# Probabilities of batches 3 to 7 turned by transposing DMAs instead of TensorE, with one exponential for a group and normalisation moved into layer two

## The chip, the cores and the metric

The kernel runs on one core of a Trainium2 chip. The metric is the device time of one execution in microseconds. Three runs of the kernel before took 315.9, 316.6 and 315.95 us, median 315.95 us. TensorE (PE) multiplies matrices and writes to PSUM, its weight loads are listed apart (PEld); VectorE (DVE) and ScalarE (ACT) work on PSUM and SBUF; GpSimd (POOL) issues the loads here, and SyncE (SP) issues the stores and the transposing DMAs.

## The reference, cut to what matters

Sliding-window attention over 8 batches, 8 heads, 576 positions and 64 channels per head, followed by two matrix products with a SiLU between them.

```python
scores = scale * np.matmul(q, k.transpose(0, 1, 3, 2))
mask_plain = (rel >= 0) & (rel < 32)
mask_dil = (rel >= 0) & (rel < 128) & (rel % 4 == 0)
masks = np.stack([mask_plain if h < 4 else mask_dil for h in range(8)], axis=0)
scores = np.where(masks[None], scores, -1e9)
scores = scores - np.max(scores, axis=-1, keepdims=True)
attn = np.exp(scores)
attn = attn / (np.sum(attn, axis=-1, keepdims=True) + 1e-9)
attn_out = np.matmul(attn, v)
x = attn_out.transpose(0, 2, 1, 3).reshape(4608, 512)
h = x @ w_in                       # w_in is 512 x 2048
out = (h / (1 + np.exp(-h))) @ w_out   # w_out is 2048 x 512
```

## The kernel before

Each batch has 576 rows. Heads 0 to 3 use a window of 32 neighbours, "plain", z = 0 in the code; heads 4 to 7 use every fourth position back to 124, "strided", z = 1. Queries are cut into blocks of 32, keys into stretches of 64, and four blocks are stacked on the 128 partitions, so a probability tile `pe` or `pn` is 128 partitions by 8 or 10 slots of 64. For each batch and z there are two such tiles, hi = 0 and hi = 1: 8 and 10 slots for z = 0, 10 and 10 for z = 1. This is what is called a group here.

A group passes through these functions. `scores` (TensorE matmuls, then on VectorE the scaling and mask into `ms` and the negated maximum of each slot into `nm`); `exps` on ScalarE (for a group without `shift`, one exponential of 64 columns for each slot with the maximum as bias, which also gives the slot's sum `l`; for a group on which `shift` was called, VectorE has subtracted the maximum in place and one exponential covers all slots, line 525); `normal` on VectorE (line 543 sums the slots if the group was shifted, then line 547 adds epsilon, line 548 takes reciprocals `r`, line 550 writes `pn` in float16); `turn` (line 559: one TensorE transpose for each pair of slots, 4 or 5 for a tile, into PSUM tile `pt`); `turned` (line 567: a copy from PSUM to the SBUF tile `ptT`); `values` (lines 592 and 656: 64 or more small matmuls of `ptT` with the values `vw`); `finish` (lines 661 to 669: copies into `xT`, the transposed input of layer one).

The main loop goes over the batches. For batch b, `layer1` runs 16 blocks of 8 matmuls (line 682) with a SiLU after each on ScalarE (line 690); then `layer2` runs 4 output tiles for an even b and 5 for an odd b, each of 16 matmuls (line 747) with a copy `ob` on VectorE (line 731) and a store on SP (line 732). Attention of the batches that follow is woven into this. The order is written out by hand: `plan_of(b)` puts calls at steps, `plan(s)` runs those of step s. Steps 0 to 15 stand ahead of the 16 blocks of layer one. Steps 16 onwards stand ahead of every fourth matmul of layer two, so output tile x has steps 16 + 4x to 19 + 4x. Every engine executes its own instructions in this program order, and waits by semaphores.

For b of 2 and more the steps before are: the plain group of batch b + 1 is normalised at step 0, turned at 4 and multiplied with its values at 6 of layer one. Strided scores of b + 1 come at step 11 (10 for b = 2) and their exponentials at 16. Plain scores of b + 2 come at 17, their exponentials at 18. The strided group of b + 1 is normalised at 22 and 24 (hi = 0 and 1), turned at 27 and multiplied at 28 (28 and 29 for b = 6). Loads of values (`load_v`, `shift_v`) and of rows of q and k (`load_rows`) are issued on POOL; `cross` (lines 140 and 147) issues transposing DMAs on SP that put those rows into `qT`, `kT`, `qC` and `kC`. Buffers that matter: `ps` (4 PSUM tiles), `big` (2 PSUM tiles), `pt` (4), `pn` and `pe` (4), `ob` (5), `vw` (2).

The SP queue issues in program order, stores and transposes alike. A store that waits for its copy holds back what stands behind it.

Of the kernel before, what the change touches and what calls it, by code (L numbers as in the profile page):

```python
# [8 lines left out]
F16 = mybir.dt.float16  # L9
# [6 lines left out]
P = 128  # L16
# [13 lines left out]
def kernel(  # L30
# [9 lines left out]
    nc = tc.nc  # L40
    B, H, S, D = q.shape
# [15 lines left out]
    WM = 12  # L57
# [8 lines left out]
    ptp = ctx.enter_context(tc.tile_pool(name="ptp", bufs=4))  # L66
# [138 lines left out]
    def plain_v(a, j, h):  # L205
        return a["vw"][j % 2 * KB : j % 2 * KB + KB, h * NM + j // 2]

    def class_v(a, j, h, r):

        e = (j if j < 4 else h // 2) % 2  # L210
        return a["vw"][e * KB : e * KB + KB, NP + j // 2 * ND + h * DIL + r]
# [18 lines left out]
    def clear_v(b, engine):  # L230
# [13 lines left out]
        out=band[0:W], in_=band[0:W], compare_op=ALU.is_ge, fill=NEG,  # L244
# [3 lines left out]
        out=band[0:W], in_=band[0:W], compare_op=ALU.is_ge, fill=NEG,  # L248
# [35 lines left out]
    def att(b):  # L284
        if b not in state:
            state[b] = {
                "qT": qTs[b % 2],
                "kT": kTs[b % 2],
                "qC": qCs[b % 2],
                "kC": kCs[b % 2],  # L290
                "vw": vws[b % 2],
                "xT": xtp.tile([P, HP, S], F16, tag="xT", name=f"xT_{b}"),
            }
        return state[b]
# [87 lines left out]
    def width(b, z, g):  # L382

        if b == 0:
            return 8 + g * (4 if z else 2)
        return 10 if z or g else 8
# [176 lines left out]
    def turned(b, z, hi, copy=nc.vector.tensor_copy):  # L563
# [2 lines left out]
        pt = a["pt", z, hi] = ptp.tile([P, WM // 2, P], F16, tag="pt", name=f"ptT_{b}_{z}_{hi}")  # L566
        copy(pt[:, 0:n], a["ptT", z, hi][:, 0:n])  # L567

    def values(b, z):

        a = att(b)
        x = a["x", z] = [
            ps.tile([P, 2, SA], F32, tag="ps", name=f"x_{b}_{z}_{e}") for e in (0, 1)
        ]
        for i in range(8):
            for n in (0, 1):
                for e in (0, 1):
                    r = slice(e * KB, e * KB + KB)
                    for hi in (0, 1):
                        dst = x[e][hi * D : hi * D + D, n]  # L580
                        pt = a["pt", z, hi]
                        if z == 0:
                            j = 2 * i + e
                            w = plain_v(a, j, 2 * n + hi)
                            dst = dst[:, i * QB : (i + 1) * QB]
                            p = pt[r, 2 * n + j // 8, i % 4 * QB : i % 4 * QB + QB]
                        else:
                            m, c = i // 4, i % 4
                            w = class_v(a, 2 * m + e, 2 * n + hi, c)
                            dst = dst[:, m * P : (m + 1) * P].rearrange("d (i r) -> d r i", r=DIL)[:, c]  # L590
                            p = pt[r, 2 * n + m, c * QB : c * QB + QB]
                        nc.tensor.matmul(dst, w, p, start=True, stop=True)  # L592
        a["xs", z] = [
            ps.tile([P, 2, QB], F32, tag="ps", name=f"xs_{b}_{z}_{e}") for e in (0, 1)
        ]
        last_values(b, z, (0, 1))
# [163 lines left out]
    def transposes(at, b, z, step):  # L760
        for which in (1, 0):
            at(step, transpose, b, z, which, both)

    def later(at, b, z, steps, copies=(nc.vector.tensor_copy, nc.vector.tensor_copy)):

        for hi in (0, 1):
            if steps[hi] is not None:
                at(steps[hi], normal, b, z, hi)
        for hi in (0, 1):
            at(steps[2], turn, b, z, hi)  # L770
        for hi in (0, 1):
            at(steps[2], turned, b, z, hi, copies[hi])
        at(steps[3], values, b, z)
        at(steps[3], finish, b, z, copies)

    def plan_of(b):
        ev = {}

        def at(s, fn, *args):
            ev.setdefault(s, []).append((fn, args))  # L780

        def all_exps(b, z):
            for hi in (0, 1):
                at(16, exps, b, z, hi)

        if b == 0:

            at(-16, normal, 0, 1, 1)
            at(-15, shift_class, 0, dve, 1, 2)
            at(-14, normal, 0, 0, 1)  # L790
            at(-13, clear_v, 1, nc.vector)
            at(-13, load_v, 1)
            for c in (2, 3):
                at(-13, load_w_out, c)
            at(-13, load_qk, 2)
            at(-8, turn, 0, 1, 1)
            at(-8, turned, 0, 1, 1, act)
            at(-6, values0, 1, 1)
            at(-6, last_values, 0, 1, (1,))
            at(-6, finish0, 1, 1)  # L800
            at(-6, last_finish, 0, 1, 1)
            at(-4, turn, 0, 0, 1)
            at(-4, turned, 0, 0, 1)
            at(-2, values0, 0, 1)
            at(-2, last_values, 0, 0, (1,))
            at(-2, finish0, 0, 1, both)
            at(-2, last_finish, 0, 0, 1)
            transposes(at, 1, 1, 2)
            at(8, scores, 1, 1)
            for hi in (0, 1):  # L810
                at(8, shift, 1, 1, hi)
            for which in (1, 0):
                at(17, transpose, 1, 0, which, (dve, dve))
            at(20, normal, 1, 1, 0)
            at(20, scores, 1, 0)
            at(14, shift_v, 1, nc.sync.dma_start)
            at(15, load_rows, 3)
            at(15, load_v, 2)
            at(15, shift_v, 2, nc.gpsimd.dma_start)
            all_exps(1, 1)  # L820
            for hi in (0, 1):
                at(20, exps, 1, 0, hi)
            for n, z, hi in ((20, 1, 1), (26, 0, 0), (28, 0, 1)):
                at(n, normal, 1, z, hi)
            for n, z, copies in ((27, 1, (dve, dve)), (30, 0, both)):
                for hi in (0, 1):
                    at(n, turn, 1, z, hi)
                for hi in (0, 1):
                    at(n, turned, 1, z, hi, copies[hi])
                at(n + 1 + z, values, 1, z)  # L830
                at(n + 1 + z, finish, 1, z, both)
        elif b == 1:
            transposes(at, 2, 0, 2)
            transposes(at, 2, 1, 10)
            at(2, cross, 3, 0)
            at(20, cross, 3, 1)
            at(28, cross, 4, 0)
            at(7, scores, 2, 0)
            at(17, load_v, 3)
            at(17, shift_v, 3, nc.gpsimd.dma_start)  # L840
            at(17, load_rows, 4)
            at(13, scores, 2, 1)
            all_exps(2, 0)
            all_exps(2, 1)
            at(21, normal, 2, 0, 0)
            at(21, scores, 3, 0)
            at(21, exps, 3, 0, 0)
            at(21, exps, 3, 0, 1)
            later(at, 2, 0, (None, 24, 27, 28))
            later(at, 2, 1, (29, 31, 33, 34))  # L850
        else:
            if b + 2 < B:
                at(16, load_v, b + 2)
                at(16, shift_v, b + 2, nc.gpsimd.dma_start)
            if b + 1 < B:
                later(at, b + 1, 0, (0, 0, 4, 6))
                if b + 3 < B:
                    at(16, load_rows, b + 3)
            if b + 2 < B:
                at(20, cross, b + 2, 1)  # L860
            if b + 3 < B:
                for n, which in ((24, 1), (28, 0)):
                    at(n, cross, b + 3, 0, (which,))
            if b + 2 < B:
                at(17, scores, b + 2, 0)
                at(18, exps, b + 2, 0, 0)
                at(18, exps, b + 2, 0, 1)
            if b + 1 < B:
                at(10 if b == 2 else 11, scores, b + 1, 1)
                all_exps(b + 1, 1)  # L870
                later(at, b + 1, 1, (22, 24, 28, 29) if b == 6 else (22, 24, 27, 28))

        def plan(s):
            for fn, args in ev.pop(s, ()):
                fn(*args)

        return plan
# [58 lines left out]
    for b in range(B):  # L936
        plan = plan_of(b)
        if b == 0:
            for x in range(NFF):
                plan(2 * x - NFF)  # L940
                plan(2 * x + 1 - NFF)
                layer1_part(2 * x % NFF, 2 * x // NFF, None if x else warm)
        else:
            for f in range(NFF):
                plan(f)
                layer1(b, f)
        if b == 0:
            layer2_first(plan)
        else:
            layer2(b, plan)  # L950
        for s in range(NFF, 3 * NFF):
            plan(s)
# [30 lines left out]
```

## Time and profile before

| What | Value |
|---|---|
| Median of 3 runs | 315.95 us |
| The profiled execution | 316.03 us, its span 314.2 us |
| PE busy | 303.2 us, 96% of the span |
| ACT busy | 205.0 us, 65% |
| DVE busy | 164.5 us, 52% |
| POOL busy | 102.9 us, 33% |
| Granted TensorE clock | 1.00 |
| Layer two of batch 2 | first matmul at 119.58 us |
| Layer one of batch 3 | first matmul at 135.64 us |

The profile is of one execution. The times between the first and last instruction are the span; the rest of the 316.03 us lies outside it. In the chain of work that ended last, a line gives a start, a length and what ran. In a timeline a line gives start, length, engine, source line and operation; consecutive instructions of VectorE overlap a little at their ends, so a start can lie before the former line's end. "To landing" is the time from the start of a DMA's issue until its last semaphore update.

### The profile page before, as it was taken

Reading aid. Unit: us, or ns where it says so; the run is one execution under the profiler, and the core shown is the slowest. Engines: PE = TensorE matmul, PEld = TensorE weight load, DVE = VectorE, ACT = ScalarE, POOL = GpSimd, SP = SyncE. Lnnn points to the kernel's source line nnn. Section 1 sums busy time; section 2 is a strip of 40 time slices with the busy share of each in tenths; the row PEclk is TensorE's granted clock in tenths of the full one; section 3 lists DMA queues with packets and bytes.
Section 4 is the critical chain, followed back from the end, with each engine's and each line's share of the span. In section 5 each row is a group of like instructions: output and inputs, shape, how many; then the busy total and the mean of one; then the engine's idle time right before and its main releaser. Section 6 shows DMA issues by size and latency. Waiting matters only on the chain.

```text
span 314.2 us, 10664 instructions
## 1 busy us (share of the span) xinstructions
PE 303.2 (96%) x4551; PEld 196.0 (62%) x4551; DVE 164.5 (52%) x356; ACT 205.0 (65%) x683; POOL 102.9 (33%) x160
## 2 busy tenths in 40 slices
PE   5889999989999999999999999999999999999995
PEld 2658754667545875577644775567644775567544
DVE  5897488626497545742574545652574442520011
ACT  1775657756999559965796458965696458636300
POOL 8535537815582391147405570051000000000000
PEclk9999999999999999999999999999999999999999
DMA  8999999999999996699949991596042000210021
GB/s 106 182 214 205 193 231 175 160 182 152 135 161 208 197 110 81 164 166 143 115 109 164 211 112 26 150 161 122 5 104 106 35 2 2 96 41 2 0 100 67
DMA packets 93504, 38.45 MB, mean 122 GB/s; under 512 B 67665, under 2 KB 88017, under 8 KB 93457
## 3 DMA queue, kind: packets, MB, share of 16 engines
q0 software_dynamic: 64160, 21.73, 63.0%
q1 hardware_dynamic: 29152, 15.98, 21.8%
q8 instruction: 35, 0.57, 0.7%
q14 instruction: 13, 0.10, 0.1%
q10 hardware_dynamic: 144, 0.07, 0.1%
HBM read 37.75 MB, written 9.44 MB: 150 GB/s over the span
## 4 chain that ended last, share of the span: by engine, by line
PE 88%; ACT 4%; DMA 3%; DVE 2%; issue 1%; POOL 1%; POOLq 0%
PE h L682 35%; PE o L747 32%; PE o L721 5%; PE h L702 4%; PE x L592 3%; PE pt L559 3%; DMA n<-in_q_dram 2%; ACT pe L534 2%; PE s L362 1%; PE s L374 1%; PE t L312 1%; PE x L618 1%; POOL n L156 1%; PE xs L656 1%; DMA out_dram<-ob 1%
## 5 line engine op out<-in xcount | busy, mean ns | idle before, releaser
L690 ACT ACTIVATE gT<-h 128x576 f16<-128x576 f32 x112 | 73.0, 652 | 65.9 <-PE h L682 65.8
L747 PE MATMUL o<-w_out,gT 128*128 128x512 f16 (+1 forms) x528 | 114.9, 373 | 0.0
L682 PE MATMUL h<-xT,w_in 128*128 128x288 f16 x896 | 114.2, 286 | 0.0
L682 PEld LDWEIGHTS <-w_in 128*128 128x128 f16 x896 | 86.2, 98 | 23.1 <-DVE xT L669 0.3
L534 ACT ACTIVATE pe<-ms,nm 128x64 f32<-128x64 f32 x246 | 81.7, 337 | 4.2 <-DVE nm L502 4.2
L747 PEld LDWEIGHTS <-gT 128*128 128x128 f16 x528 | 50.4, 98 | 53.8
L731 DVE COPY ob<-o 128x512 f32<-128x512 f32 (+1 forms) x34 | 23.2, 682 | 58.8 <-PE o L747 57.8
L534 ACT ACTIVATION_READ_ACCUMULATOR pe<-ms,nm 128x1 f32 x246 | 47.0, 191 | 0.0
L486 DVE SCALAR_TENSOR_TENSOR ms<-s,mask 128x512 f32<-128x512 f32 x28 | 19.2, 686 | 45.1 <-PE s L374 25.0
L165 POOL DMA_DIRECT2D vw<-in_v_dram x16 | 10.0, 638 | 49.5 <-PE x L592 49.4
L550 DVE TENSOR_TENSOR pn<-pe,r 128x640 f16<-128x640 f32 (+2 forms) x32 | 25.3, 792 | 1.1
L669 DVE CAST xT<-x 128x512 f16<-128x512 f32 x26 | 16.8, 686 | 12.0 <-PE xs L656 12.0
L502 DVE TENSOR_REDUCE nm<-ms 128x10 f32<-128x640 f32 (+1 forms) x28 | 22.0, 787 | 1.0
L702 PE MATMUL h<-xT,w_in 128*128 128x256 f16 (+1 forms) x128 | 17.9, 296 | 0.5 <-ACT gT L709 0.5
L567 DVE COPY ptT<-pt 128x640 f16<-128x640 f16 (+1 forms) x28 | 12.1, 469 | 8.7 <-PE pt L559 8.7
L702 PEld LDWEIGHTS <-w_in 128*128 128x128 f16 x128 | 12.6, 101 | 4.6 <-issue 1.2
L721 PE MATMUL o<-w_out,gT 128*128 128x512 f16 x64 | 15.2, 380 | 0.2 <-issue 0.2
L119 POOL DMA_DIRECT2D n<-in_k_dram x20 | 14.9, 761 | 1.4 <-issue 1.3
L709 ACT ACTIVATE gT<-h 128x512 f16<-128x512 f32 (+1 forms) x16 | 10.3, 651 | 7.0 <-PE h L702 6.9
L119 POOL DMA_DIRECT2D n<-in_q_dram x20 | 14.8, 789 | 0.0
L559 PE MATMUL pt<-ident,pn 128*128 128x128 f16 x152 | 12.0, 224 | 0.4 <-DVE pn L550 0.4
L559 PEld LDWEIGHTS <-pn 128*128 128x128 f16 x152 | 10.1, 100 | 3.3 <-DVE pn L550 0.6
(108 smaller groups left out, 249.1 us busy)
## 6 DMA issues: line engine op xcount, KB each, us to landing
out_dram<-ob SPq DMA_DIRECT2D x35, 256.0 KB, 3.3
vw<-in_v_dram POOLq DMA_DIRECT2D x8, 288.0 KB, 8.0
vw<-in_v_dram POOLq DMA_DIRECT2D x16, 128.0 KB, 4.7
w_in<-in_moe_w_in_dram POOLq DMA_DIRECT2D x4, 512.0 KB, 11.9
w_out<-in_moe_w_out_dram POOLq DMA_DIRECT2D x4, 512.0 KB, 10.6
n<-in_k_dram POOLq DMA_DIRECT2D x6, 256.0 KB, 4.7
n<-in_q_dram POOLq DMA_DIRECT2D x6, 256.0 KB, 5.6
vw<-vw POOLq DMA_DIRECT2D x12, 128.0 KB, 3.3
```

The source lines that it names most:

```text
L119: nc.gpsimd.dma_start(out=f[:, h // 2, :, h % 2], in_=src[b, h].rearrange("(m p) d -> p m d", p=RT))
L486: nc.vector.scalar_tensor_tensor(out=ms[:, 0:8].rearrange("p (n t) c -> p n (t c)", n=2), in0=s[hi].rearrange("p n t c -> p n (t c)"), sca ...
L502: nc.vector.tensor_reduce(out=nm[:, 0:w], in_=ms[:, 0:w], axis=AX.X, op=ALU.max, negate=True)
L534: nc.scalar.activation(pe[:, t, :], slot(t), AF.Exp, scale=1.0 if b else scale, bias=nm[:, t : t + 1], accum_out=l[:, t : t + 1],)
L550: nc.vector.tensor_tensor(pn[:, 0:w], a["pe", z, hi][:, 0:w], r[:, 0:w, None].broadcast_to([P, w, KB]), ALU.mult)
L559: nc.tensor.transpose(t[:, i, :], a["pn", z, hi][:, 2 * i : 2 * i + 2].rearrange("p t c -> p (t c)"), ident)
L682: nc.tensor.matmul(h[:, half, 0:HS], w_in16[:, c, f * P : f * P + P], xT[:, c, half * HS : half * HS + HS], start=(c == 0), stop=(c == MC ...
L690: nc.scalar.activation(gT[:, f, s0 : s0 + S].rearrange("p (a c) -> p a c", a=2), h[:, :, 0:HS], AF.Silu)
L702: nc.tensor.matmul(h[:, i, 0 : c1 - c0], w_in16[:, c, (f + i) * P : (f + i + 1) * P], xT[:, c, c0:c1], start=(c == 0), stop=(c == MC - 1),)
L721: nc.tensor.matmul(o, gT[:, f, t * P : (t + 1) * P], w_out16[:, f, :], start=(f == 0), stop=(f == NFF - 1),)
L731: copy(ob, o)
L747: nc.tensor.matmul(o, gT[:, f, t * P : (t + 1) * P], w_out16[:, f, m0:m1], start=(f == 0), stop=(f == NFF - 1),)
```

## The change

For batches 3 to 7, `turn` and `turned` go away. A new function issues one transposing DMA on SP for each probability tile, straight from `pn` to `ptT`. The DMA has to wait for `pn`, and `values` for the DMA.

The strided group of b + 1 is still normalised at steps 22 and 24, each followed by its DMA, and `values` moves from 28 to 29. The plain group of b + 2 is normalised at steps 27 and 30 of layer two, each followed by its DMA, and `values` comes at step 4 of the next layer one. Batch 3's plain group is normalised and turned by DMA at step 0 of b = 2, and multiplied at 6. The hi = 1 tile of the strided group now has `shift` at step 11, so one exponential of 640 columns replaces ten of 64, and `normal` sums the slots on VectorE. In iteration 1, both tiles of batch 2's plain group are shifted in the same way at step 8, scores stand one step later, the exponentials of batch 3's plain group move from step 21 to 24. `cross` moves: the strided rows from step 20 to 16, the plain rows from 24 and 28 to 31.

```diff
+    def turn_by_dma(b, z, hi):
+
+        a = att(b)
+        w = width(b, z, hi)
+        pt = a["pt", z, hi] = ptp.tile([P, WM // 2, P], F16, tag="pt", name=f"ptT_{b}_{z}_{hi}")
+        nc.sync.dma_start_transpose(
+            out=pt[:, 0 : w // 2], in_=a["pn", z, hi][:, 0:w].rearrange("p t c -> p (t c)")
+        )
...
             transposes(at, 2, 0, 2)
-            transposes(at, 2, 1, 10)
+            transposes(at, 2, 1, 11)
...
-            at(7, scores, 2, 0)
+            at(8, scores, 2, 0)
+            for hi in (0, 1):
+                at(8, shift, 2, 0, hi)
...
-            at(13, scores, 2, 1)
+            at(14, scores, 2, 1)
...
-            at(21, exps, 3, 0, 0)
-            at(21, exps, 3, 0, 1)
             later(at, 2, 0, (None, 24, 27, 28))
+            at(24, exps, 3, 0, 0)
+            at(24, exps, 3, 0, 1)
             later(at, 2, 1, (29, 31, 33, 34))
         else:
             if b + 2 < B:
+                at(16, cross, b + 2, 1)
                 at(16, load_v, b + 2)
                 at(16, shift_v, b + 2, nc.gpsimd.dma_start)
+            if b + 3 < B:
+                at(16, load_rows, b + 3)
             if b + 1 < B:
-                later(at, b + 1, 0, (0, 0, 4, 6))
-                if b + 3 < B:
-                    at(16, load_rows, b + 3)
-            if b + 2 < B:
-                at(20, cross, b + 2, 1)
-            if b + 3 < B:
-                for n, which in ((24, 1), (28, 0)):
-                    at(n, cross, b + 3, 0, (which,))
+                if b == 2:
+                    for hi in (0, 1):
+                        at(0, normal, 3, 0, hi)
+                        at(0, turn_by_dma, 3, 0, hi)
+                at(6 if b == 2 else 4, values, b + 1, 0)
+                at(6 if b == 2 else 4, finish, b + 1, 0)
+                at(11, scores, b + 1, 1)
+                at(11, shift, b + 1, 1, 1)
+                all_exps(b + 1, 1)
             if b + 2 < B:
                 at(17, scores, b + 2, 0)
-                at(18, exps, b + 2, 0, 0)
-                at(18, exps, b + 2, 0, 1)
+                for hi in (0, 1):
+                    at(18, exps, b + 2, 0, hi)
             if b + 1 < B:
-                at(10 if b == 2 else 11, scores, b + 1, 1)
-                all_exps(b + 1, 1)
-                later(at, b + 1, 1, (22, 24, 28, 29) if b == 6 else (22, 24, 27, 28))
+                for hi in (0, 1):
+                    at(22 + 2 * hi, normal, b + 1, 1, hi)
+                    at(22 + 2 * hi, turn_by_dma, b + 1, 1, hi)
+                at(29, values, b + 1, 1)
+                at(29, finish, b + 1, 1)
+            if b + 2 < B:
+                for hi in (0, 1):
+                    at(27 + 3 * hi, normal, b + 2, 0, hi)
+                    at(27 + 3 * hi, turn_by_dma, b + 2, 0, hi)
+            if b + 3 < B:
+                at(31, cross, b + 3, 0)
```

## The prediction

> **What bounds the kernel now.** I read the page's busy table first, then the chain of work that ended last, then the chain's pieces over batches 2 and 3.
>
> ```profile
> PE 303.2 (96%) x4551; PEld 196.0 (62%) x4551; DVE 164.5 (52%) x356; ACT 205.0 (65%) x683; POOL 102.9 (33%) x160
> ...
> PE 88%; ACT 4%; DMA 3%; DVE 2%; issue 1%; POOL 1%; POOLq 0%
> ```
>
> ```profile
> 121.29 8.74 PE o L747 x40
> 130.03 0.56 PE pt L559 x10
> 130.59 0.86 PE o L747 x4
> 131.46 0.64 PE x L592 x64
> 132.10 0.14 PE xs L656 x16
> 132.24 3.56 PE o L747 x16
> ```
>
> TensorE is never idle here: piece follows piece. Whatever TensorE no longer does is gained in full, and whatever TensorE must wait for is lost in full. No other engine has a price of its own. So I look for what the new wait of `values` costs.
>
> Next, VectorE in the same stretch, which must finish `pn`, and the two kinds of transposing DMA on SP from 124 to 240 us (columns: shortest, median, longest issue in ns; below them the time from issue to landing).
>
> ```profile
> 127.48 0.69 DVE L731 COPY ob<-o 128x512 f32<-128x512 f32 x1 [1.00 <-PE o L747]
> 128.52 0.17 DVE L547 TENSOR_SCALAR r<-l 128x10 f32<-128x10 f32 x1 [0.35 <-ACT pe L534]
> 128.73 0.22 DVE L548 RECIPROCAL r<-r 128x10 f32<-128x10 f32 x1
> 128.98 0.82 DVE L550 TENSOR_TENSOR pn<-pe,r 128x640 f16<-128x640 f32 x1
> ```
>
> ```profile
> L147 SPq DMA_TRANSPOSE kC<-n x8: 1173/1224/1301, 125.5 to 232.1; - x8
> ...
> DMA to landing us min/median/max: 2.3/2.7/2.8
> ```
>
> ```profile
> L140 SPq DMA_TRANSPOSE kT<-n x6: 1220/1650/2462, 131.4 to 204.2; - x6
> ...
> DMA to landing us min/median/max: 4.2/5.7/8.4
> ```
>
> The first kind runs while POOL loads nothing, the second from the moment the next values are loaded. The same instruction takes 2.3 to 2.8 us in quiet and 4.2 to 8.4 us beside loads.
>
> **Removed from TensorE.** Five batches lose ten transposes (0.56 us in the chain, as above) and nine (0.50 us, at 139.72 us and alike in the others): 5 x 1.06 = 5.3 us gained. VectorE's copies `ptT` (0.4 to 0.5 us each) go too; VectorE is 52% busy, so nothing comes of it by itself.
>
> **Strided group, steps 22 to 29, five times.** `normal` of hi = 1 stands at step 24, in program order behind the copy `ob` of output tile 1, which waits for that tile's last matmul. In layer two of batch 2 this copy starts at 127.48 us. An independent VectorE operation behind a 0.69 us one starts 0.60 us later (the pair at 122.61 and 123.21 us), so the new slot sum starts at 128.08. It takes 0.82 us (813 ns in its row of the page's groups, 128x10 from 128x640), to 128.90. Then lines 547, 548 and 550 need 1.28 us, as from 128.52 to 129.80 above: `pn` is ready at about 130.21, SP issues at 130.26.
> The landing is unknown for 128x5x128. In quiet the 128x8x128 transpose of 125.47 us issued for 1.27 us, moved 1,024 rows of 256 bytes until about 1.0 us after that, and had landed 2.75 us after its start. With 5 of 8 tiles the middle part is 0.64 us: 2.35 us, which I take, as it is nearest in kind. Lower end 1.9 us, if the issue shrinks by 5/8 also; upper end 2.75 us. Landed and seen: 132.66.
> TensorE arrives at step 29 after 48 matmuls of 0.216 us from 121.23 us (first matmul behind the plain scores), with 0.1 us for the switch of shape: 131.70. So it waits 0.95 us, five times: 4.75 us (ends 2.5 and 6.75). The tile hi = 0 has `pn` at 126.5 us and is hidden. The single exponential (732 ns for 128x640 in line 525's row, against 3.3 us for ten) saves ScalarE 2.6 us, but ScalarE waits for TensorE, 65.8 us of it at line 690, so this is worth nothing; the subtraction that it adds on VectorE (0.82 us in layer one) is hidden by VectorE's idle time there.
>
> **Plain group of batch 3.** It has no earlier place: `pn` is ready at 103.54 and 104.74 us in the trace of before, SP is held 1.25 us by the first transpose, so the second starts at 104.85. POOL is loading values then. Stores issued at 100.94 and 102.53 us landed after 5.3 and 4.8 us, the quickest transpose beside loads took 4.2: I take 4.5, landing 109.35, seen 109.4. TensorE comes to step 6 at 101.61 + 6 x 0.98 + 0.1 = 107.6: a wait of 1.8 us (0 with 2.75 us, 3.8 with 6.5 us).
>
> **Plain groups of batches 4 to 7.** `pn` of hi = 1 follows the copies into `xT`. From the end t of the values: copies 1.5 us, normalisation 1.28 us, issue at t + 2.8. TensorE needs it at step 4, after 12 matmuls (2.6 us) and 4 blocks (3.9 us): t + 6.6 for even b. Up to 3.75 us of landing is hidden. POOL starts its loads at t, in bursts; the first `kT` beside them landed after 4.2 to 4.5 us, one in quiet would after 2.35. I take 4.0, which gives 0.2 us each for batches 4 and 6: 0.4 us together (0 and 7.4). For odd b four more steps of layer two hide 7.2 us: nothing (upper end 1.2 us each).
>
> **Iteration 1.** VectorE's order is `ob`, the slot sum of hi = 0, its `pn`, the masks of batch 3, `ob`, the slot sum of hi = 1, its `pn`. ScalarE's earlier end pays for the first sum: in the trace VectorE waited 0.6 us for `pe` there. The second sum adds 0.73 us (820 ns less overlap) ahead of `pn`, while line 547 shrinks by 0.16: TensorE's turn at 90.66 us, which already waited 0.6 us for `pn`, waits 0.55 us more (0 and 1). Shifts at step 8 lie in idle time of VectorE.
>
> **The queue.** SP now issues four more transposes of 1.2 us an iteration, 4.9 us of some 35. Behind a waiting transpose stand stores; five `ob` buffers cover a delay of some microseconds. Strided `cross` moves ahead of POOL's loads into layer one, its readers come at step 11 of the next iteration. Plain `cross` at step 31 is read at step 17, over 15 us later. Both cost nothing unless SP hangs back by a layer.
>
> **Sum.** -5.3 + 4.75 + 1.8 + 0.4 + 0.55 = +2.2 us on the profiled execution's 316.03 (span 314.2, 1.8 around it): 318.2. That execution lies 0.08 us over the median of 315.95, which changes no digit that matters.
>
> [...] Beside loads the traces show transposes landing up to 8.4 us after issue. [...]
>
> **Rivals.**
> [...]
> Faster: the issue shrinks with the tile count. Then a quiet landing takes 1.9 us, each strided wait is 0.5 us, and the plain landings lose the same 0.45: 2.5 + 1.35 + 0 + 0.55 - 5.3 = -0.9, 315.1; with a gap in the loads for batch 3, 313.8. It decides once the quiet landing is under some 1.95 us. Against it: 128x8x16, an eighth of the data, still issued for 1.17 us and landed after 2.3.
> Heavy queues: plain transposes land as the `qT` ones beside loads did (six of them, 6.1 to 8.4 us; I take 7): batch 3 waits 4.3 us, batches 4 and 6 3.2 us each: -5.3 + 4.75 + 4.3 + 6.4 + 0.55 = +10.7, 326.7 us. For it: qT issued at 135.63, about when the new one would be, took 7.5 us. Against it: that one stood behind two `kT`, which now come after.
> The change not doing what it says: the transposes leave TensorE by construction; only the waits are open.
>
> **How the numbers follow.** A difference of 0.3% (0.95 us) is about what a measurement tells from none. My sum 0.45 (317 to 320.5), fair turns 0.15 (same), faster 0.20, heavy queues 0.20 (320.5 to 327, fewer the higher). So faster 0.20, same 0.15, slower 0.65. The time is 318.2; the range 314.2 to 323.2 leaves out about half of the faster case and half of the heavy one.
>
> **What would show it.** In the profile after: L559 has 57 instead of 152 transposes; TensorE has a gap of about 0.95 us ahead of `values` in layer two of batches 2 to 6, ended by a DMA `ptT`; one of some 1.8 us at block 6 of batch 2; the new DMA lands 2.2 to 2.5 us after issue in quiet. If the gaps in layer two are under 0.5 us or the DMA is quicker than 2 us, I am wrong to the fast side; if gaps at block 4 of batches 3 and 5 exceed 1.5 us, to the slow side.

## The result and the profile after

The changed kernel takes 329.0 us (median of four runs, 326.97 to 332.25) against 315.92 us for the kernel before in the same job: a ratio of 1.0388 with a 95% interval of 1.0338 to 1.0438. The forecast was 318.2 us with a range up to 323.2. The sign was right, the size was not: +13 us came, +2.2 were forecast.

The ratio leaves out the profiled execution, which at 332.25 us (span 330.5) is the longest of the four and 3.3 us above their median, so its waits are a little long; the lower clock is not its own alone (0.978, against 0.972 to 0.983 in the other three). First the page of the changed kernel: the busy row, the granted TensorE clock in 40 slices of 8.26 us, and the chain that ended last by engine.

```profile
PE 304.7 (92%) x4456; PEld 194.7 (59%) x4456; DVE 166.3 (50%) x350; ACT 186.4 (56%) x554; POOL 102.7 (31%) x160
...
PEclk9999999999999789999999999995999999999999
...
PE 79%; DMA 12%; DVE 3%; ACT 3%; issue 1%; POOL 1%; POOLq 0%
```

TensorE has 95 matmuls fewer and yet no less busy time than before (304.7 against 303.2 us). DMA holds 12% of the chain in place of 3%, and the clock row shows three slices below 9. The page of before has none.

The instructions and waits around the tile `ptT` in the changed kernel, for the new DMA alone (durations of the issue in ns, who waited for it in us and times, then the time from issue to landing):

```profile
L574 SPq DMA_TRANSPOSE ptT<-pn x20: 1193/1207/1232, 104.0 to 287.9; - x20
...
  PE x L601: 14.9, 9
...
DMA to landing us min/median/max: 2.3/2.4/7.7
```

TensorE waits for the new DMA nine times, 14.9 us in all. The median landing is the 2.35 us of the forecast; the longest is three times that.

**Strided groups.** TensorE in layer two of batch 2 of the changed kernel (start, length, what ran, and in brackets the idle time ahead):

```profile
138.88 0.21 PE L601 MATMUL x<-ptT,vw 64*64 64x32 f16 x1
139.91 0.70 PE L601 MATMUL x<-ptT,vw 64*64 64x32 f16 x63 [0.82 <-DMA ptT<-pn]
```

From the first matmul, which needs hi = 0 only, to the second one, which needs hi = 1, it is 1.03 us. The other four places have 1.01 or 1.02. This is the 0.95 of the forecast.

**Plain group of batch 3.** TensorE in layer one of batch 2, changed kernel:

```profile
105.80 1.51 PE L691 MATMUL h<-xT,w_in 128*128 128x288 f16 x11
110.93 0.17 PE L601 MATMUL x<-ptT,vw 64*64 64x32 f16 x1 [3.62 <-DMA ptT<-pn]
113.01 1.04 PE L601 MATMUL x<-ptT,vw 64*64 64x32 f16 x63 [1.91 <-DMA ptT<-pn]
...
114.09 7.04 PE L691 MATMUL h<-xT,w_in 128*128 128x288 f16 x40
```

The two turns were issued at 103.98 and 105.28 us and landed after 6.90 and 7.68 us, so TensorE stands still from 107.2 to 113.0 but for one matmul, 5.75 us beyond its usual pace. And then 40 matmuls of layer one take 7.04 us. The same 40 in the kernel before, in layer one of batch 5:

```profile
213.51 0.69 PE L592 MATMUL x<-ptT,vw 64*64 64x32 f16 x64
...
214.19 5.07 PE L682 MATMUL h<-xT,w_in 128*128 128x288 f16 x40
```

The windows of the changed kernel say why (columns: stretch, us, PE busy with count, granted clock, DMA share, GB/s):

```profile
107.00:111.30 4.30, 0.48 (x4) 1.00 1.40 123
111.40:118.10 6.70, 5.09 (x88) 0.50 1.74 198
118.20:121.00 2.80, 2.80 (x24) 1.00 1.45 129
...
224.00:230.70 6.70, 6.34 (x94) 0.50 1.21 192
```

The clock falls inside the long wait, at 111.3 us, and is 0.50 for 6.8 us; TensorE works for 5.1 us of these. (The last row is from the wait of batch 6, below.) In batch 3 the fall follows 3.7 us without the start of a matmul (107.24 to 110.93 us) and then a single one; in batch 6, at 223.94 us, it comes 3.4 us after the last matmul ended. The clock is back after 6.83 us both times, 5.1 and 6.3 us of them work. What sets these lengths no run shows. The prediction did not think of it.

**Plain group of batch 6**, layer one of batch 5, changed kernel:

```profile
220.36 0.20 PE L601 MATMUL x<-ptT,vw 64*64 64x32 f16 x1
224.36 1.04 PE L601 MATMUL x<-ptT,vw 64*64 64x32 f16 x63 [3.80 <-DMA ptT<-pn]
...
225.44 9.63 PE L691 MATMUL h<-xT,w_in 128*128 128x288 f16 x56
```

The same picture: 4.0 us of waiting, then 56 matmuls in 9.63 us, where they take 7.03 at full clock (in the experiment with the filled wait). The plain group of batch 4 waited 1.79 us (landing 5.39 us after its issue) and lost no clock; that of batch 5 needed 6.23 us and was covered by the fifth output tile.

The difference of the two profiled executions, 330.48 - 314.23 = 16.25 us, by the starts of the stages:

| Step of the forecast | Forecast | Measured |
|---|---|---|
| Transposes gone from TensorE | -5.3 | -5.3 (0.50 less in each layer one without a wait: 17.37 against 17.87) |
| Five strided waits | +4.75 | +5.0 |
| Plain, batch 3 | +1.8 | +8.0: 5.75 of wait, 1.97 of half clock in the 40 matmuls, the rest in the slower small ones |
| Plain, batches 4 and 6 | +0.4 | +1.8 and +7.0 (4.0 of wait, 2.6 of half clock in the 56 matmuls, the rest in the small ones) |
| Iteration 1 and all before batch 2 | +0.55 | -0.3 (+0.7 in the wait for `pn`, the rest elsewhere) |
| Sum | +2.2 | +16.2 |

### The profile page after: what moved, and what is told of

Its sections match the earlier page's. It is cut to its first block, busy times and chain, and to the rows that moved or that the text cites. A ratio compares the mean times of both kernels' runs of the same rounds, so it can differ in the third digit from the quotient of the medians.

```text
span 330.5 us, 10385 instructions
## 1 busy us (share of the span) xinstructions
PE 304.7 (92%) x4456; PEld 194.7 (59%) x4456; DVE 166.3 (50%) x350; ACT 186.4 (56%) x554; POOL 102.7 (31%) x160
## 3 DMA queue, kind: packets, MB, share of 16 engines
q0 software_dynamic: 64160, 21.73, 61.3%
q1 hardware_dynamic: 41952, 19.10, 26.9%
## 4 chain that ended last, share of the span: by engine, by line
PE 79%; DMA 12%; DVE 3%; ACT 3%; issue 1%; POOL 1%; POOLq 0%
PE h L691 32%; PE o L756 29%; DMA ptT<-pn 10%; PE o L730 4%; PE h L711 4%; PE x L601 3%; DMA n<-in_q_dram 2%; PE s L374 1%; PE s L362 1%; PE t L312 1%; PE pt L559 1%; ACT pe L534 1%; PE x L627 1%; POOL n L156 1%; PE xs L665 1%
## 5 line engine op out<-in xcount | busy, mean ns | idle before, releaser
L691 PE MATMUL h<-xT,w_in 128*128 128x288 f16 x896 | 117.9, 293 | 0.0
L691 PEld LDWEIGHTS <-w_in 128*128 128x128 f16 x896 | 88.5, 100 | 25.9 <-DVE xT L678 0.3
L534 ACT ACTIVATE pe<-ms,nm 128x64 f32<-128x64 f32 x178 | 59.1, 333 | 4.2 <-DVE nm L502 4.1
L534 ACT ACTIVATION_READ_ACCUMULATOR pe<-ms,nm 128x1 f32 x178 | 33.1, 186 | 0.0
L601 PE MATMUL x<-ptT,vw 64*64 64x32 f16 x896 | 12.0, 192 | 14.9 <-DMA ptT<-pn 14.9
L601 PEld LDWEIGHTS <-vw 64*64 64x64 f16 x896 | 9.9, 114 | 20.7 <-issue 20.7
L711 PEld LDWEIGHTS <-w_in 128*128 128x128 f16 x128 | 12.8, 103 | 4.4 <-issue 0.8
L186 POOL DMA_DIRECT2D vw<-vw x6 | 2.9, 489 | 22.6 <-DMA vw<-in_v_dram 22.6
```

The costliest lines, as they stand in the source:

```text
L534: nc.scalar.activation(pe[:, t, :], slot(t), AF.Exp, scale=1.0 if b else scale, bias=nm[:, t : t + 1], accum_out=l[:, t : t + 1],)
L691: nc.tensor.matmul(h[:, half, 0:HS], w_in16[:, c, f * P : f * P + P], xT[:, c, half * HS : half * HS + HS], start=(c == 0), stop=(c == MC ...
L711: nc.tensor.matmul(h[:, i, 0 : c1 - c0], w_in16[:, c, (f + i) * P : (f + i + 1) * P], xT[:, c, c0:c1], start=(c == 0), stop=(c == MC - 1),)
```

## The experiments

Theory after the result: the turns that are issued while POOL loads values land late, because of the loads; the rest is the half clock. Rivals: the strided waits, the single exponential, or the order on SP.

**One part alone.** The plain groups are turned on TensorE as before, the strided ones by DMA.

```diff
-                if b == 2:
-                    for hi in (0, 1):
-                        at(0, normal, 3, 0, hi)
-                        at(0, turn_by_dma, 3, 0, hi)
-                at(6 if b == 2 else 4, values, b + 1, 0)
-                at(6 if b == 2 else 4, finish, b + 1, 0)
+                later(at, b + 1, 0, (0, 0, 4, 6))
...
-                for hi in (0, 1):
-                    at(27 + 3 * hi, normal, b + 2, 0, hi)
-                    at(27 + 3 * hi, turn_by_dma, b + 2, 0, hi)
```

> The plain groups of batches 3 to 7 are turned on TensorE again (normalised at step 0, turned at 4, values at 6, as before); the strided ones stay with DMAs. Theory: all of the loss beyond some 2 us comes from the plain groups, whose DMAs share the queues with the loads of values, and from the half clock after their long waits. Then 5 strided waits of 1.0 us against 5 turns of 0.56 us saved: 315.9 + 2.2 - 0.3 (iteration 1, as the trace of the changed kernel has it) = 317.8 us, clock 1.00. Rival: transposing DMAs hold up SP and the rest of the queues in any place, half of the loss stays: 322 us or more.

Measured: 320.63 us, ratio 1.013 (1.0084 to 1.0176). The waits of TensorE in this kernel (us in total, times, longest):

```profile
PE x L601 <- DMA ptT<-pn: 4.1, 5, 0.9
...
PE s L374 <- issue: 3.1, 3, 1.4
```

The five strided waits are there, but the kernel is 2.8 us over the expectation, and what stands beside it is called "issue": TensorE waits for nothing that the profile shows. More of that below.

The other part alone: strided groups back on TensorE, plain ones by DMA.

```diff
-                for hi in (0, 1):
-                    at(22 + 2 * hi, normal, b + 1, 1, hi)
-                    at(22 + 2 * hi, turn_by_dma, b + 1, 1, hi)
-                at(29, values, b + 1, 1)
-                at(29, finish, b + 1, 1)
+                later(at, b + 1, 1, (22, 24, 28, 29) if b == 6 else (22, 24, 27, 28))
```

> The other half alone: the strided groups are turned on TensorE at 27, values at 28 (28 and 29 for b = 6), the plain ones by DMA as in the changed kernel. Theory: the changed kernel's 327 to 329 us less 5 x 0.44 = 325 to 327 us, clock still 0.97 to 0.98. Rival: the two halves disturb one another through the SP queue, and one alone goes well: under 320 us.

Measured: 330.11 us, ratio 1.0417 (1.036 to 1.0474), no better than the whole change. From issue to landing its ten turns take

```profile
DMA to landing us min/median/max: 2.5/5.7/8.4
```

The expectation was 325 to 327 us, so this is missed by 3 us: with the strided groups back on TensorE nothing was regained in the total. The plain groups carry the loss.

**The half clock by itself.** Twelve matmuls of 512 columns on idle data stand ahead of the plain values in the layer one of batches 2 and 5; they fill part of the wait and move nothing else.

```diff
+                if b in (2, 5):
+                    at(6 if b == 2 else 4, fill, 12)
                 at(6 if b == 2 else 4, values, b + 1, 0)
```

> The changed kernel with 12 matmuls of 128x512 on an unused PSUM tile (12 x 0.216 = 2.6 us) ahead of the plain values in layer one of b = 2 and b = 5, inside the waits of 5.7 and 4.3 us. Theory of the clock: the idle stretch gets shorter than what makes the clock fall to 0.50, the waits end when they did, and the slow matmuls behind them (2.0 and 2.6 us lost) go: 328 - 4.6 = 323.4 us, mean clock 0.99 or more. Rival: the time behind the waits was lost to something else, such as buffers: 328 us as before, or more.

Measured: 326.66 us, ratio 1.0307 (1.0235 to 1.0379), against 323.4 expected. The timeline of TensorE in this kernel, first for batch 3, then for batch 6, and a window from the stretch that had a clock of 0.50:

```profile
107.16 2.75 PE L911 MATMUL fill<-ident 128*128 128x512 f16 x12
109.88 0.17 PE L601 MATMUL x<-ptT,vw 64*64 64x32 f16 x1
111.10 0.68 PE L601 MATMUL x<-ptT,vw 64*64 64x32 f16 x63 [1.05 <-DMA ptT<-pn]
...
111.78 5.07 PE L691 MATMUL h<-xT,w_in 128*128 128x288 f16 x40
```

```profile
220.46 7.03 PE L691 MATMUL h<-xT,w_in 128*128 128x288 f16 x56
```

```profile
113.50:118.00 4.50, 4.50 (x112) 1.00 2.10 119
```

The 40 and the 56 matmuls are back at 5.07 and 7.03 us, the clock at 1.00: the half clock follows from the idle wait, and costs 1.97 + 2.60 us in these matmuls. The profiled execution, 324.68 us, is below the median here; in it the landings were also shorter (batch 3: 6.56 and 6.48 us), so not all of the 7.6 us to the profiled execution of the change are the clock's. The medians differ by 2.3 us only.

**What holds the landings.** First without any loads and shifted copies of values for batches 4 to 7.

```diff
-                at(16, load_v, b + 2)
-                at(16, shift_v, b + 2, nc.gpsimd.dma_start)
```

> The changed kernel without the loads of values for batches 4 to 7 and the shifted copies made of them (lines 165 to 198 from b = 2 on); the matmuls then use the values of batches 2 and 3. TensorE's instructions are the same, one for one. Theory: the plain DMAs land late because of these loads. Without them they land after 2.3 to 2.5 us, as the strided ones do; batch 3 waits 0.5 us, batches 4 and 6 not at all, the clock stays at 1.00: 315.9 - 5.3 + 5.0 + 0.5 + 0.7 (iteration 1) = 316.8 us. Rival: the transposes on SP hold one another up (four for q and k stand behind each plain pair); landings stay over 5 us, the time over 324 us. A side question: TensorE's waits named issue sum to 4.9 and 8.4 us in the two runs that came out slower than expected, against 2.2 before. If they are instruction blocks that come late beside loads, they fall to 2 us here.

Measured: 326.38 us, ratio 1.0261 (1.0174 to 1.0349), against 316.8 expected. The new DMA in this kernel between 98 and 116 us, and between 210 and 235:

```profile
L574 SPq DMA_TRANSPOSE ptT<-pn x2: 1226/1833/2440, 102.7 to 105.3; - x2
DMA to landing us min/median/max: 8.8/9.0/9.3
```

```profile
L574 SPq DMA_TRANSPOSE ptT<-pn x3: 1205/1207/1309, 210.8 to 216.8; - x3
DMA to landing us min/median/max: 2.3/2.4/2.7
```

In the later batches the theory holds: without the loads the plain turns land like quiet ones, and the waits of batches 4 and 6 are gone (layer one of batch 5 takes 17.49 us instead of 24.36). Batch 3 became worse, and that the theory had not foreseen: with its value work gone POOL comes to the loads of q and k rows sooner, at 93 to 106 us where they were issued at 111 to 119, and those arrive in pieces of 128 bytes too. What harms is not values as such.

So next only one load was left out, the one of line 178, which brings the plain values in pieces of 128 bytes.

```diff
-                at(16, load_v, b + 2)
+                at(16, load_v, b + 2, ("first", "second", "short"))
```

> The changed kernel without one of the five value loads, that of line 178 (36 x 64 pieces of 128 bytes), for batches 4 to 7. Theory: this one, with 2304 short packets, holds the transposes up: landings of the plain DMAs fall to 2.4 to 4 us, time 317 to 319 us. Rival: the longer packets (512 bytes of lines 165 and 173, 4096 of the shifted copies) do as much: landings stay over 5 us, time 324 us or more.

Measured: 318.92 us (ten runs), ratio 1.0039 (0.9994 to 1.0085). The turns of batch 3 in it:

```profile
L574 SPq DMA_TRANSPOSE ptT<-pn x2: 1195/1286/1378, 105.2 to 106.5; - x2
DMA to landing us min/median/max: 4.2/4.2/4.2
```

The turn of batch 4 lands after 3.65 us, that of batch 5 after 2.65 in place of 6.23. One load of 288 KB for each of four batches, with its 128-byte pieces, makes ten microseconds of the change's thirteen. SP's order is the same in both kernels. The DMA queues of the changed kernel from 104 to 106.9 us show what it does (q0 carries POOL's loads, 64,160 packets on the pages of before and after; q1 what SP issues, 29,152 before and 41,952 after; packets, MB, share of 16 engines):

```profile
q0 software_dynamic: 1947, 0.32, 145.5%
q1 hardware_dynamic: 192, 0.31, 29.8%
```

Nearly two thousand small packets of q0 run in these 2.9 us, and only 8 of the 256-byte packets of the turn that was issued at 103.98; those came from 107 us on, some 300 to 390 a microsecond. That q0 goes first is read from this trace, not tested by itself.

**The single exponential.** Without the shift of the strided hi = 1, ten exponentials again, and VectorE has no slot sum ahead of `pn`.

```diff
-                at(11, shift, b + 1, 1, 1)
```

> The changed kernel without the shift at step 11, so that the strided hi = 1 group has ten exponentials again and no slot sum in normal. Theory: the slot sum (0.82 us) stands in the chain copy of tile 1, sum, normalisation, DMA, values; without it ScalarE's tenth exponential sets the start, 128.52 in the trace of before, where the sum let it start at 128.93. The strided waits fall from 1.0 to about 0.6 us. Rival: nothing changes there, since VectorE is late for another reason: 1.0 us.

Measured: 325.82 us, one execution. The strided gaps shrink to 0.58 to 0.63 us in four places, as expected: the sum on VectorE ahead of `pn` costs 0.4 us each. The fifth, in layer two of batch 6, grows to 1.39. The plain gaps stay (3.65 + 1.59, 1.20, 3.05 us), so the exponential is not the cause of the loss.

**Values later.** If only the landing is late, `values` can come later: plain ones at step 14, strided ones at 30.

```diff
-                at(6 if b == 2 else 4, values, b + 1, 0)
-                at(6 if b == 2 else 4, finish, b + 1, 0)
+                at(14, values, b + 1, 0)
+                at(14, finish, b + 1, 0)
...
-                at(29, values, b + 1, 1)
-                at(29, finish, b + 1, 1)
+                at(30, values, b + 1, 1)
+                at(30, finish, b + 1, 1)
```

> The changed kernel, with the plain values moved from steps 4 and 6 to 14 and the strided ones from 29 to 30. Theory: every landing then lies under TensorE's work. The plain ones have 8 to 10 us more, which covers the longest seen (7.7 us); the strided ones 0.87 us more, against a wait of 1.0: 0.1 us left each. 315.9 - 5.3 + 0.5 - 0.3 = 310.8 us, clock 1.00. Rival: the later values collide with the masks on VectorE (four PSUM tiles are shared with the strided scores of step 11) or keep the next layer one waiting for its input: 313 us or more.

Measured: 320.69 us, ratio 1.0137 (1.009 to 1.0184). The theory's 310.8 us was missed by ten; the rival's "313 us or more" came true, but its reasons (VectorE, the next layer one's input) account for 1.4 us at most, the waits for `ob`. All landings are hidden now; the waits of TensorE in this kernel are others:

```profile
PE x L601 <- issue: 2.1, 2, 1.1
PE s L362 <- issue: 2.0, 1, 2.0
PE h L691 <- DVE ob L740: 1.4, 2, 0.7
...
PE o L756 <- issue: 1.0, 1, 1.0
```

One of them in its timeline, in the middle of 64 equal matmuls whose operands were all there:

```profile
152.74 0.55 PE L601 MATMUL x<-ptT,vw 64*64 64x32 f16 x45
154.43 0.33 PE L601 MATMUL x<-ptT,vw 64*64 64x32 f16 x19 [1.14 <-issue]
```

I numbered TensorE's instructions in the traces (matmuls, weight loads and the few others of its queue, such as waits for a semaphore, in order of start, from 0). For five of the kernels, the last instruction ahead of each "issue" gap of over 0.9 us behind instruction 2000, with the gap from start to start in us:

```
kernel                      number (gap)
before                      2496 (1.17)
after                       2752 (0.98)
plain on TensorE            2752 (1.32)  4032 (1.64)
values 14, 30               2496 (2.17)  4288 (0.94)  5056 (1.32)  5312 (1.35)  6080 (1.15)
without line 178's load     2240 (1.02)  2496 (1.35)  5312 (1.22)
```

Every number is 192 more than a multiple of 256 (why 192 stays open). The traces of before and after also show 35 transfers of 16,384 bytes each on an instruction queue of their own (the pages' q8: 35 packets, 0.57 MB), one for about every 256 of TensorE's 9,125 and 8,931 instructions. In the kernel with 14 and 30 one starts at 152.1 us, the gap begins at 153.1 and ends at 154.4. My reading, from these counts and places alone: each transfer brings a block of 256 instructions, and where TensorE is through with its 256 before the next block has come, it waits. Scores and values are quick ones: with the values at 14, close behind the scores at 11, blocks pass in 3.9 to 4.2 us, while in the kernel before, with layer-one matmuls between them, none takes under 4.87. The limit is not sharp: gaps follow blocks of 4.9 to 8.0 us too, where the transfer started late, 3.5 to 5.8 us behind the last border.

To test this, the same kernel with 72 narrow transposes on idle data in iteration 1, ahead of the turn that waits there anyway. They move every later block border by 144 instructions, and no work.

```diff
+        for _ in range(72 if (b, z, hi) == (2, 0, 1) else 0):
+            nc.tensor.transpose(t[:, 0, 0:32], ident[0:32], ident[0:32, 0:32])
         for i in range(width(b, z, hi) // 2):
```

> The values at steps 14 and 30, with 72 narrow transposes more on TensorE (144 instructions with their weight loads) in iteration 1, ahead of the turn that waits there 1.41 us anyway; what they write is overwritten. Theory (instructions come in blocks): with the values at 14 and 30 alone every stall of over 0.9 us named issue stands at a TensorE instruction whose number is 192 more than a multiple of 256 (2496, 4288, 5056, 5312, 6080), and it stands where a whole block of 256 passes in under about 5.3 us. Moved by 144, hardly a block after 95 us passes so fast (the shortest in that trace would take 5.6 us), so the stalls at 121.96, 153.11, 160.12 and 192.00 go (4.8 us, with the small ones up to 7); the 72 cost about 1.9 us less the wait of 1.41. Time 314 to 317, about 315.5, against 320.7. Rival (the stalls belong to the work at their places, a semaphore or a port): they stay at the same matmuls, time about 321.

Measured: 314.56 us (nine runs), ratio 0.9952 (0.9925 to 0.9979). It does more work than the kernel without them and is 6 us faster. The extra instructions, and the values that had a gap in their middle, in its timeline:

```profile
90.37 1.96 PE L559 MATMUL pt<-ident 32*128 32x32 f16 x72
...
151.06 0.68 PE L603 MATMUL x<-ptT,vw 64*64 64x32 f16 x64
```

None of the four gaps after 95 us is left. Instead of moving the borders, the work can be pulled apart: strided scores from step 11 to 5, plain values from 14 to 12.

```diff
-                at(14, values, b + 1, 0)
-                at(14, finish, b + 1, 0)
-                at(11, scores, b + 1, 1)
-                at(11, shift, b + 1, 1, 1)
+                at(12, values, b + 1, 0)
+                at(12, finish, b + 1, 0)
+                at(5, scores, b + 1, 1)
+                at(5, shift, b + 1, 1, 1)
```

> The values at 14 and 30 with the strided scores moved from step 11 to 5 and the plain values from 14 to 12, so that seven layer-one tiles stand between them. Theory (blocks): no block is made of scores and values alone, so the stalls of the iterations at 153.11, 160.12 and 192.00 go (3.8 us); the landings of the plain turns are hidden still, but for batch 3 (landed about 13 steps after its issue: 0 to 1 us). Time about 316 to 317.5. Rival (the stalls belong to the work): about 320.7 as with 14 and 30.

Measured: 313.99 us (ten runs), ratio 0.9932 (0.9898 to 0.9966), better than expected. No "issue" gap of over 0.5 us is left after 76 us.

A third use of the same idea, the first experiment with its strided values at step 30:

```diff
-                at(29, values, b + 1, 1)
-                at(29, finish, b + 1, 1)
+                at(30, values, b + 1, 1)
+                at(30, finish, b + 1, 1)
```

> Plain groups turned on TensorE as before, strided groups by DMA with their values at step 30 in place of 29. With step 29 the five waits for the landing took 5.11 us; one step later is 0.87 us of matmuls, so 0.15 us each is left at most. Theory (each wait is a plain term): 320.6 - 4.4 = 316.2, within 0.3% of before. Rival (the waits hid other work, blocks of instructions or VectorE): 318 or more, with the time back under issue or pn.

Measured: 317.8 us, ratio 1.0033 (0.9998 to 1.0067), between the two. No wait for the strided turns is left in TensorE's list, but gaps stand at 4032 (2.09 us) and 7104 (1.29 us), both 192 beyond a multiple of 256. Behind the first one the clock fell too, for 3.4 us, although the wait was short:

```profile
113.00:116.40 3.40, 1.50 (x85) 1.00 1.55 128
116.50:119.80 3.30, 3.30 (x16) 0.50 0.53 115
```

**The order on SP.** The kernel with 14 and 30, with the strided `cross` back at step 20, where it was before.

```diff
-                at(16, cross, b + 2, 1)
...
+                at(20, cross, b + 2, 1)
```

> The kernel with plain values at 14 and strided ones at 30, and with the strided cross back at step 20, so that its four transposes leave the stretch in which POOL loads. TensorE's instructions are those of the kernel that took 320.7 us, one for one. Theory: the waits named issue there (8.4 us) are instruction blocks fetched late beside transposes and loads; with 590 KB less in that stretch they fall by half, 316 to 317 us. Rival: the loads alone make them late, or they fall anyhow: 320 us. The DMAs of strided hi = 0 come 1 to 3 us later on SP, those of hi = 1 not over 0.5 us.

Measured: 326.03 us, ratio 1.0275 (1.0207 to 1.0344); both sides missed. SP's queue in this kernel, in layer two of batch 2:

```profile
124.64 2.57 SPq L147 DMA_TRANSPOSE kC<-n  x2
127.32 2.51 SPq L147 DMA_TRANSPOSE qC<-n  x2
129.94 1.22 SPq L574 DMA_TRANSPOSE ptT<-pn  x1
131.25 0.53 SPq L741 DMA_DIRECT2D out_dram<-ob  x1
131.91 2.55 SPq L574 DMA_TRANSPOSE ptT<-pn  x2
```

`pn` of hi = 0 was ready at 125.7 us, that of hi = 1 at 129.5, and their turns were issued at 129.94 and 131.91: the four row transposes take SP 5.2 us. TensorE then waits 1.94 us for hi = 1 in place of none, and about as long in three later places. Behind three of these four waits the clock falls as well, to 0.50 for 3.4 us each; here the first:

```profile
135.20:138.50 3.30, 3.30 (x9) 0.50 0.86 156
```

This kernel numbers TensorE's instructions as the one with 14 and 30 does, its blocks pass in 3.9 us as well, and none of the gaps of over 0.9 us is in its trace: the transfers start sooner there, for the gap of 153.1 us 0.5 us behind the last border in place of 3.1. So how early the next transfer starts counts too. That the four row transposes delay it where they stand at step 16 fits, but it rests on one trace. As for `cross`, its move to step 16 is a part of the change that pays: 320.69 us with it, 326.03 without.

**The best version found.** With 14 and 30 and the 144 instructions, layer one of batches 3 and 5 waited 0.97 us for the last copy `ob`, which stood on VectorE behind `normal` of step 30.

```diff
-                    at(27 + 3 * hi, normal, b + 2, 0, hi)
-                    at(27 + 3 * hi, turn_by_dma, b + 2, 0, hi)
+                    at(27 + 2 * hi, normal, b + 2, 0, hi)
+                    at(27 + 2 * hi, turn_by_dma, b + 2, 0, hi)
```

> As with the 144 instructions and the values at 14 and 30, with the plain group's second half normalised and turned at step 29 in place of 30. At 30 it stands on VectorE behind the four copies of the strided output and ahead of the copy of the last layer-two tile, and layer one waits for that copy 0.97 and 0.96 us (batches 3 and 5). VectorE is idle 1.6 us ahead of those copies, and the half takes 1.45. Theory: both waits go, time 314.56 - 1.7 = 312.9, a ratio to before of about 0.990. Rival (the exponentials of that half are not ready a step earlier, so VectorE waits for ScalarE and the copies come later): 314.5 or more.

Measured: 312.37 us, ratio 0.9875 (0.9828 to 0.9921): faster than both kernels. In its waits neither `ob` nor the turns stand above 0.2 us; one gap of 1.76 us is left, at instruction 4288, again 192 beyond a multiple of 256.

## Why the prediction was right or wrong

**The gain on TensorE** (-5.3) was right, and so were **the strided waits** (0.95 forecast, 1.01 to 1.03 measured), down to the landing in quiet (2.35 forecast, 2.38 to 2.41 measured, one of 3.27). By the experiment with ten exponentials, VectorE's slot sum makes 0.4 us of each.

**The plain group of batch 3** is the step that failed first: "the quickest transpose beside loads took 4.2: I take 4.5". It took 6.90 and 7.68 us. **The plain groups of batches 4 to 7** failed in the same way: 4.0 us were taken, 5.39, 6.23 and, for batch 6, about 7.6 measured. That the odd batches hide it was right. Instead of the middle of the rows beside loads, 5.7 (`kT` alone 4.2 to 5.4, `qT` 6.1 to 8.4), I took their quick end, on the argument that the slow ones stood behind others on SP. SP was not what held the turns: line 178's load was, which is issued at 101.8 us, just ahead of them; without it those of batch 3 landed after 4.2 us. The prediction also read the rows from 124 us on only. Nearer to the turn of batch 3, at 104 us, the trace of before has these:

```profile
L140 SPq DMA_TRANSPOSE kT<-n x2: 1237/1336/1436, 93.8 to 95.5; - x2
L140 SPq DMA_TRANSPOSE qT<-n x2: 1715/1938/2160, 96.8 to 98.7; - x2
...
DMA to landing us min/median/max: 5.9/6.6/7.9
```

Their median of 6.6 us would have given a wait of 3.9 us in place of 1.8.

**The rival of heavy queues** (326.7 us, chance 0.20) had the right mechanism and nearly the right waits: 4.3 and twice 3.2, 10.7 us, against 5.75 + 1.79 + 4.0 = 11.5. What takes the time beyond it is the half clock, which was no part of any case and had no term in the sum: 4.6 us in the layer-one matmuls and some 0.7 in the small ones. The range ended at 323.2, in the middle of that rival.

**Fair turns** (same, chance 0.15): no run shows that case. The turns beside all the loads landed after 5.39 to 7.68 us, and TensorE waited 5.75 us for batch 3 alone.

**Iteration 1** (+0.55 forecast, +0.7 measured in the wait) and **the queue** ("both cost nothing") held; the experiment with `cross` at 20 shows that its old place would have cost.

A wait of TensorE was taken as lost in full, and the two long ones cost more than their length. The statement that TensorE "is never idle here" left out the gaps called "issue": with every landing hidden the kernel came out at 320.7 us, and the gain appeared only when the blocks fell elsewhere (314.56 us with the 144 instructions).

## What to carry to other kernels

A transposing DMA in place of TensorE's transposes paid here where its landing was hidden and the blocks fell well (312.37 us in the best version, a ratio to before of 0.9875), and its landing must be read from transfers issued in the same stretch beside the same loads, at the slow end of those rows: 2.4 us in quiet, 5.4 to 9.3 beside 128-byte loads here. TensorE's waits of 5.75 and 4.0 us cost their length and then half the speed (a granted clock of 0.50) for 5.1 and 6.3 us of work. When small matmuls are moved together, count instructions: in the kernel with 14 and 30, blocks of 256 that passed in 3.9 to 4.2 us ended in gaps of TensorE, and moving the border or putting large matmuls between brought the time back, from 320.69 to 314.56 and 313.99 us.

## What was not expected of the hardware

- One load of 288 KB a batch in 128-byte pieces turned landings of 2.65 to 4.2 us into 5.4 to 7.7.
- The granted clock fell to 0.50 for 6.8 us after waits of 5.75 and 4.0 us. It also fell, for 3.4 us, after waits of 2.1 us (instruction 4032, strided values at 30), 1.9 us (`cross` at 20) and 0.6 and 1.05 us one behind the other (scores at 5, near 131.9 us), while a gap of 2.17 us (at instruction 2496 with 14 and 30) and one of 1.79 us (batch 4 of the changed kernel) left it at 1.00. What decides after short waits stays open.
- All 16 gaps over 0.9 us called "issue" behind instruction 2000, in the 14 traces of this case, stand at 192 beyond a multiple of 256, 0.94 to 2.17 us each. 144 instructions more made a kernel 6 us faster.
